# Packed attention, SwiGLU and a bilinear layer on one core: weight sums in more steps, with loads at other places of the queue

## The chip, the cores and the metric

The kernel runs on one core of a Trainium2 chip. The metric is the device time of one launch in microseconds (us), as the median of several runs. All five engines of the core work on one program: TensorE (PE, with its weight loads PEld), VectorE (DVE), ScalarE (ACT), GpSimd (POOL) and SyncE (SP), and every transfer between device memory and the core's buffers is issued from SP's one queue.

## What is computed

```python
p_packed = softmax_attention(p, k, v)          # 8 batches, 8 heads, 32 packed rows, head size 64
a = softmax_attention(q, p_packed, p_packed)   # 576 rows per batch, 4608 tokens of 512 in all
xn = a / rms(a) * rms_g
h = silu(xn @ w_gate) * (xn @ w_val)           # 512 -> 1536
y = h @ w_out                                  # 1536 -> 512
out = ((y @ w1) * (y @ w2)) @ w3 @ w_out2      # 512 -> 1024 -> 1024 -> 512
```

Every large product is done with operands cut into a high and a low float32r part, as three products (high by high, low by high, high by low). The product w3 @ w_out2 is folded into one matrix beforehand, and y @ w1 and y @ w2 are done with seven block products in place of eight (a Strassen-like scheme), for which sums and differences of weight blocks and of y's blocks are needed.

## The kernel before

The program has three stages, one behind the other on TensorE.

**Attention and h.** Up to about 528 us the attention, the norm and h are computed, batch by batch, and h is stored transposed in device memory (`hT_d`).

**y and the preparation of the second layer.** y is computed in nine tiles of 512 tokens by `y_part(t, tag)` (line 557). I call them tile 0 to tile 8. A tile has 12 steps (one per 128 rows of w_out), and a step is 12 matmuls (line 566, four PSUM banks by three products). In step n of all tiles the kernel also issues the load of the h row n+4 (`fetch_h`, tile `hr`, five buffers) and splits row n+2 (`split_h`): ScalarE writes the high part `hh` (line 55), VectorE the low part `hl` (line 56), each with three buffers. So the split of a row can start when the row three ahead of it has been multiplied, and must be done two steps later. At a tile's end two evictions each on ScalarE and VectorE write `y`, which goes to `y_d` three steps later (`store_later`, `stores`).

Between tiles stand the two halves of the folded product, `folded(0)` after tile 2 and `folded(1)` after tile 4 (96 matmuls each, line 657), which read the converted and split w3 and w_out2.

Beside the tiles other work is handed out by `together(main, total, *others)`: each of the others is a generator with a number of pieces, and a first and a last place as shares of the main work; after each step at most one piece is taken, from whichever is furthest behind. The order in which the instructions are written is the order in each engine's queue; nothing is reordered later. The pieces beside tiles 5 to 7 are those of `layer2()`, 33 of them: 16 conversions of 64-bit weight blocks (`w64` loaded, ScalarE and VectorE two operations each, GpSimd one at line 114) and four groups of sums. A group takes four converted blocks a11, a12, a21, a22 (tiles `c_o`), forms sums and differences of them in place on GpSimd (lines 608 to 616), splits seven results into a staging buffer with `put` (high part on ScalarE, low part on VectorE, 128x512 each) and stores them as four transfers of 896 KB to `ws_d`. There are two staging buffers, `stage0` and `stage1`.

Then come, at the top level of the program:

```python
    together(chained(y_part(5, "gv"), y_part(6, "at"), y_part(7, "gv")), 36.0, (33, layer2(), 0.0, 0.97))
    flush()
    p2_ctx.close()
    ...
    fetch_y(0)
    load_w(0)
    together(y_part(NTILE - 1, "at"), 12.0, (8, sums(0), 0.0, 0.85), (4, last_loads(0), 0.1, 0.9))
```

`flush()` issues all stores still held. `p2_ctx.close()` gives the staging buffers' memory to new tiles. `fetch_y(0)` loads y tiles 0 and 1 (`yi`, 1 MB each) and `load_w(0)` the first slice of the summed weights (`w`, 1.8 MB). `sums(0)` (line 709) forms y's sums for the first pair of tiles, with parts `xh` on ScalarE and `xl` on VectorE (two of seven on GpSimd); these tiles lie where the staging buffers lay, so their first writes wait for the last stores out of `stage1`. `last_loads(n)` loads and splits four blocks of the folded matrix (`w34_h`, `w34_l`).

**The second layer.** `run(p)` (line 780) works through pairs of y tiles: for each of eight slices i, seven block products (42 matmuls, line 799), and the products into the output (line 772). ScalarE copies the first product's bank to `p1` (line 805) before TensorE may add to that bank. In the first pair, each slice ends with one piece of `last_loads(1)`.

Of the kernel before, what the change touches and what calls it, by code (L numbers as in the profile page):

```python
# [13 lines left out]
ALU = mybir.AluOpType  # L14
# [18 lines left out]
def packed_attention_swiglu_bilinear(ctx: ExitStack, tc, qT, kT, v, pT, rms_g, w_gv, w_out,  # L33
                                     w1, w2, w3T, w_out2, out):
    nc = tc.nc
# [561 lines left out]
    def group(g):  # L597
# [5 lines left out]
        def put(j, src, eng):  # L603
            hi, lo = (to[:, :, j, s, :] for s in range(2))
            split(hi, lo, src.rearrange("p (i n) -> p i n", i=4), eng)

        put(3, a22, nc.vector)
        nc.gpsimd.tensor_tensor(out=a22, in0=a21, in1=a22, op=ALU.add)
        put(0, a11, nc.vector)
        nc.gpsimd.tensor_tensor(out=a21, in0=a11, in1=a21, op=ALU.subtract)  # L610
        yield
        nc.gpsimd.tensor_tensor(out=a11, in0=a22, in1=a11, op=ALU.subtract)
        put(1, a12, nc.vector)
        put(4, a22, nc.vector)
        yield
        nc.gpsimd.tensor_tensor(out=a12, in0=a12, in1=a11, op=ALU.subtract)
        put(6, a21, nc.vector)
# [57 lines left out]
    late = chained(late, last_split())  # L675
    together(chained(y_part(3, "at"), y_part(4, "gv"), folded(1, "at")), 32.0, (8, late, 0.0, 0.7))
    together(chained(y_part(5, "gv"), y_part(6, "at"), y_part(7, "gv")), 36.0, (33, layer2(), 0.0, 0.97))
    flush()
    p2_ctx.close()
    cv2_ctx.close()  # L680

    wt = ctx.enter_context(tc.tile_pool(name="wt", bufs=1, side="right"))
    pairs = [(t, t + 1) for t in range(0, NTILE - 1, 2)] + [(NTILE - 1,)]
    ys, xs, ws = {}, {}, {}

    def fetch_y(p):
        if p < len(pairs):  # L690
# [54 lines left out]
    def last_loads(n):  # L745
        for kk in range(4 * n, 4 * n + 4):
            split(w34_h[kk], w34_l[kk], fetch(w34_d[128 * kk:128 * kk + 128, :]), nc.gpsimd)
            yield

    fetch_y(0)  # L750
    load_w(0)
    together(y_part(NTILE - 1, "at"), 12.0, (8, sums(0), 0.0, 0.85), (4, last_loads(0), 0.1, 0.9))
    flush()
# [26 lines left out]
    def run(p):  # L780
# [7 lines left out]
        for i in range(8):  # L788
# [98 lines left out]
```

## Time and profile before

| | |
|---|---|
| median of 3 runs | 1455.12 us (1455.07 to 1457.11) |
| the profiled execution | 1451.91 us |
| its span, first to last instruction | 1450.1 us |
| TensorE busy | 1360.0 us, 94% |
| VectorE, ScalarE, GpSimd busy | 55%, 38%, 34% |
| transfers' share of the 16 DMA engines | 49.5% |
| mean granted TensorE clock | 0.981 |

The profile shows one execution. TensorE is busy almost throughout, so the places that matter are the few at which it waits. They are found in the timeline of its instructions, where a wait stands in brackets behind the instruction that ended it, and by laying the starts of equal pieces of work beside each other: two tiles with the same 144 matmuls should take equally long.

### The profile page before, as it was taken

Reading aid. Unit: us, or ns where it says so; the run is one execution under the profiler, and the core shown is the slowest. Engines: PE = TensorE matmul, PEld = TensorE weight load, DVE = VectorE, ACT = ScalarE, POOL = GpSimd, SP = SyncE. Lnnn points to the kernel's source line nnn. Section 1 sums busy time; section 2 is a strip of 40 time slices with the busy share of each in tenths; the row PEclk is TensorE's granted clock in tenths of the full one; section 3 lists DMA queues with packets and bytes.
Section 4 is the critical chain, followed back from the end, with each engine's and each line's share of the span. In section 5 each row is a group of like instructions: output and inputs, shape, how many; then the busy total and the mean of one; then the engine's idle time right before and its main releaser. Section 6 shows DMA issues by size and latency. Waiting matters only on the chain.

```text
span 1450.1 us, 22603 instructions
## 1 busy us (share of the span) xinstructions
PE 1360.0 (94%) x8824; PEld 1121.8 (77%) x8824; DVE 795.9 (55%) x1267; ACT 546.7 (38%) x1080; POOL 489.9 (34%) x438
## 2 busy tenths in 40 slices
PE   4579999999999899999999978999999999999988
PEld 2368878778788788888887756888788788788877
DVE  4787576666766557736358844335334433533343
ACT  3455455555555555624245532113112211311211
POOL 2456445445456542201034503322221222222111
PEclk9689999999999999999999999999999999999999
DMA  9854453444222466726349885442642633444263
GB/s 308 296 186 119 160 186 120 154 153 141 75 96 81 153 211 236 229 98 201 121 161 364 313 307 225 167 149 84 238 146 88 237 141 115 179 142 145 92 254 125
DMA packets 65562, 253.65 MB, mean 175 GB/s; under 512 B 7344, under 2 KB 7344, under 8 KB 55344
## 3 DMA queue, kind: packets, MB, share of 16 engines
q1 hardware_dynamic: 65456, 252.21, 49.5%
q8 instruction: 69, 1.13, 0.3%
q14 instruction: 37, 0.30, 0.1%
HBM read 185.08 MB, written 67.11 MB: 174 GB/s over the span
## 4 chain that ended last, share of the span: by engine, by line
PE 75%; DVE 8%; DMA 5%; ACT 3%; issue 3%; POOL 1%; SPq 1%; ACTq 0%; DVEq 0%; POOLq 0%
PE gv L799 22%; PE gv L376 17%; PE at L566 8%; PE gv L772 7%; PE at L772 7%; PE gv L566 6%; PE at L337 2%; DMA hr<-w_d 2%; DMA w<-ws_d 2%; PE at L657 2%; PE gv L657 2%; DVE stage L56 1%; PE at L292 1%; DVE c_t L111 1%; DVE th L383 1%
## 5 line engine op out<-in xcount | busy, mean ns | idle before, releaser
L799 PE MATMUL gv<-xh,w 128*128 128x512 f32 (+1 forms) x1120 | 288.7, 373 | 13.5 <-DMA w<-ws_d 6.1
L55 ACT ACTIVATE hh<-hr 128x512 fp32r<-128x512 f32 (+1 forms) x148 | 91.2, 618 | 421.1 <-DVE hr L767 332.9
L799 PEld LDWEIGHTS gv<-xh,w 128*128 128x128 f32 x1120 | 201.9, 190 | 53.3 <-DMA w<-ws_d 7.4
L388 POOL TENSOR_TENSOR ht<-th,vl 128x288 f32<-128x288 f32 x192 | 163.8, 861 | 178.6 <-ACT vl L387 97.6
L376 PE MATMUL gv<-ah,wbh 128*128 128x288 f32 x768 | 178.6, 314 | 15.9 <-ACT vl L387 12.4
L56 DVE TENSOR_TENSOR hl<-hr,hh 128x512 fp32r<-128x512 f32 (+1 forms) x148 | 140.4, 951 | 63.2 <-ACT hh L55 60.2
L376 PEld LDWEIGHTS gv<-ah,wbh 128*128 128x128 f32 x768 | 122.7, 191 | 67.6 <-issue 27.8
L826 POOL TENSOR_TENSOR u<-u,c 128x512 f32<-128x512 f32 (+1 forms) x40 | 63.5, 1587 | 323.5 <-DVE u L767 323.5
L376 PE MATMUL gv<-al,wbh 128*128 128x288 f32 x768 | 167.2, 299 | 0.0
L767 DVE TENSOR_TENSOR hr<-gv,hr 128x512 f32<-128x512 f32 (+1 forms) x80 | 51.1, 639 | 209.4 <-PE gv L799 209.4
L376 PE MATMUL gv<-ah,wbl 128*128 128x288 f32 x768 | 165.5, 297 | 0.0
L799 PE MATMUL gv<-xl,w 128*128 128x512 f32 (+1 forms) x560 | 162.3, 372 | 0.0
L114 POOL TENSOR_TENSOR c_o<-c_o,c_y 128x512 int32<-128x512 int32 x52 | 72.9, 1402 | 223.1 <-DVE c_o L112 200.6
L376 PEld LDWEIGHTS gv<-al,wbh 128*128 128x128 f32 x768 | 125.1, 190 | 1.1 <-DVE al L56 0.9
L376 PEld LDWEIGHTS gv<-ah,wbl 128*128 128x128 f32 x768 | 124.8, 190 | 0.0
L383 DVE SCALAR_TENSOR_TENSOR th<-th,gv 128x288 f32<-128x288 f32 x192 | 84.3, 445 | 63.1 <-ACT th L382 62.1
L799 PEld LDWEIGHTS gv<-xl,w 128*128 128x128 f32 x560 | 102.6, 191 | 18.4
L566 PE MATMUL at<-hh,wo_h 128*128 128x512 f32 x240 | 94.7, 394 | 7.3 <-ACT hh L55 7.3
L387 ACT ACTIVATE vl<-gv 128x288 f32<-128x288 f32 x192 | 79.3, 413 | 58.5 <-PE gv L376 57.2
L56 DVE TENSOR_TENSOR wbl<-at,wbh 128x512 fp32r<-128x512 f32 x96 | 65.9, 687 | 60.3 <-ACT wbh L55 59.6
L566 PE MATMUL at<-hl,wo_h 128*128 128x512 f32 x240 | 94.8, 395 | 2.3 <-DVE hl L56 2.1
L382 ACT ACTIVATE th<-gv 128x288 f32<-128x288 f32 x192 | 79.4, 413 | 42.9 <-PE gv L376 42.9
(131 smaller groups left out, 2416.2 us busy)
## 6 DMA issues: line engine op xcount, KB each, us to landing
w<-ws_d SPq DMA_DIRECT2D x40, 1792.0 KB, 7.4
hT_d<-ht SPq DMA_DIRECT2D x96, 288.0 KB, 2.5
hr<-hT_d SPq DMA_DIRECT2D x108, 256.0 KB, 4.4
ws_d<-stage SPq DMA_DIRECT2D x16, 896.0 KB, 8.3
w<-in_w_gv_dram SPq DMA_DIRECT2D x24, 512.0 KB, 7.0
w<-in_w_out_dram SPq DMA_DIRECT2D x20, 512.0 KB, 4.5
v<-in_v_dram SPq DMA_DIRECT2D x8, 1152.0 KB, 7.6
q<-in_qT_dram SPq DMA_DIRECT2D x8, 1152.0 KB, 7.0
```

Of the source, the lines that this page charges most:

```text
L55: nc.scalar.activation(out=hi, in_=src, func=AF.Copy)
L56: eng_lo.tensor_tensor(out=lo, in0=src, in1=hi.bitcast(F32), op=ALU.subtract)
L114: nc.gpsimd.tensor_tensor(out=d, in0=d, in1=shape(y), op=ALU.add)
L376: nc.tensor.matmul(t[:, :HALF], lhsT=w[:, e, 256 * i + 128 * f:256 * i + 128 * f + 128], rhs=x[:, e, HALF * hf:HALF * hf + HALF], start=(n ...
L382: nc.scalar.activation(out=th, in_=t[:, :HALF], func=AF.Tanh, scale=0.5)
L383: nc.vector.scalar_tensor_tensor(out=th, in0=th, scalar=1.0, in1=t[:, :HALF], op0=ALU.add, op1=ALU.mult)
L387: nc.scalar.activation(out=vl, in_=t[:, :HALF], func=AF.Copy, scale=0.5)
L388: nc.gpsimd.tensor_tensor(out=ht[:, hf], in0=th, in1=vl, op=ALU.mult)
L566: nc.tensor.matmul(acc[m], lhsT=w[:, kk, 128 * m:128 * m + 128], rhs=x, start=(kk == 0 and a == 0), stop=(kk == NF - 1 and a == 2))
L772: nc.tensor.matmul(acc[m], lhsT=x[:, 128 * m:128 * m + 128], rhs=w[i], start=(i == 0 and n == 0), stop=(i == 7 and n == 2))
L799: nc.tensor.matmul(t, lhsT=wi[:, r, j, a], rhs=x[b][:, j, r, :w], start=(start and n == 0), stop=(n == 5), skip_group_check=True)
L826: nc.gpsimd.tensor_tensor(out=u2, in0=u2, in1=c22, op=ALU.mult)
```

## The change

Three things are edited. (1) In `group`, the seven puts and four GpSimd operations are cut into five pieces in place of four, and a put stands a piece behind the GpSimd operation that it reads. (2) The second half of the folded product moves from behind tile 4 to behind tile 3, with the last conversions for it beside tile 3; `layer2` (now 37 pieces) starts with six pieces beside the second half of tile 4, and its other 31 end at 0.9 of tiles 5 to 7. The loads of `fetch_y(0)` are handed out as one piece at 0.3 to 0.4 of these tiles, and the `flush()` before tile 8 is gone, so that stores still held go out between the next loads. (3) `load_w(0)` becomes a piece of tile 8 at 0.3 to 0.4; `last_loads` issues each load one piece ahead of the split that uses it (five pieces), and in the first pair it starts at the second slice.

```diff
         put(3, a22, nc.vector)
         nc.gpsimd.tensor_tensor(out=a22, in0=a21, in1=a22, op=ALU.add)
+        yield
         put(0, a11, nc.vector)
         nc.gpsimd.tensor_tensor(out=a21, in0=a11, in1=a21, op=ALU.subtract)
-        yield
         nc.gpsimd.tensor_tensor(out=a11, in0=a22, in1=a11, op=ALU.subtract)
+        yield
+        put(4, a22, nc.vector)
         put(1, a12, nc.vector)
-        put(4, a22, nc.vector)
-        yield
         nc.gpsimd.tensor_tensor(out=a12, in0=a12, in1=a11, op=ALU.subtract)
+        yield
         put(6, a21, nc.vector)
         put(5, a11, nc.vector)
         yield
...
-    together(chained(y_part(3, "at"), y_part(4, "gv"), folded(1, "at")), 32.0, (8, late, 0.0, 0.7))
-    together(chained(y_part(5, "gv"), y_part(6, "at"), y_part(7, "gv")), 36.0, (33, layer2(), 0.0, 0.97))
-    flush()
+    together(chained(y_part(3, "at"), folded(1, "gv")), 20.0, (8, late, 0.0, 0.55))
...
+    second = layer2()
+    together(y_part(4, "at"), 12.0, (6, some(second, 6), 0.5, 1.0))
+    together(chained(y_part(5, "gv"), y_part(6, "at"), y_part(7, "gv")), 36.0, (31, second, 0.0, 0.9),
+             (1, (fetch_y(0) for _ in range(1)), 0.3, 0.4))
...
     def last_loads(n):
-        for kk in range(4 * n, 4 * n + 4):
-            split(w34_h[kk], w34_l[kk], fetch(w34_d[128 * kk:128 * kk + 128, :]), nc.gpsimd)
-            yield
-
-    fetch_y(0)
-    load_w(0)
-    together(y_part(NTILE - 1, "at"), 12.0, (8, sums(0), 0.0, 0.85), (4, last_loads(0), 0.1, 0.9))
+        kks = list(range(4 * n, 4 * n + 4))
+        x = fetch(w34_d[128 * kks[0]:128 * kks[0] + 128, :])
+        yield
+        for kk in kks:
+            nx = fetch(w34_d[128 * kk + 128:128 * kk + 256, :]) if kk != kks[-1] else None
+            split(w34_h[kk], w34_l[kk], x, nc.gpsimd)
+            x = nx
+            yield
+
+    def first_w():
+        load_w(0)
+        yield
+
+    together(y_part(NTILE - 1, "at"), 12.0, (8, sums(0), 0.0, 0.85), (5, last_loads(0), 0.1, 0.9),
+             (1, first_w(), 0.3, 0.4))
...
-            if p == 0:
+            if p == 0 and i > 0:
                 next(rest, None)
```

Three places show what this does to the queues. The first is SP's queue where tile 7 ends and tile 8 begins; `hr<-hT_d` is a load of one h row, `hr<-w34_d` of a block of the folded matrix. Before:

```order
L356 DMA ws_d_67<-stage1_6939 128x1792 x4
L356 DMA y_d_66<-y_9519 128x2048
L694 DMA yi_9534<-y_d_66 128x2048
L694 DMA yi_9536<-y_d_66 128x2048
L703 DMA w_9538<-ws_d_67 128x3584
L497 DMA hr_9542<-hT_d_63 128x512
L497 DMA hr_9564<-hT_d_63 128x512
L497 DMA hr_9585<-hT_d_63 128x512
```

And now:

```order
L356 DMA ws_d_67<-stage1_6939 128x1792
L497 DMA hr_9488<-hT_d_63 128x512
L356 DMA ws_d_67<-stage1_6939 128x1792
L497 DMA hr_9507<-hT_d_63 128x512
L497 DMA hr_9537<-hT_d_63 128x512
L356 DMA ws_d_67<-stage1_6939 128x1792
L497 DMA hr_9560<-hT_d_63 128x512
L356 DMA ws_d_67<-stage1_6939 128x1792
L497 DMA hr_9582<-hT_d_63 128x512
L356 DMA y_d_66<-y_9525 128x2048
L497 DMA hr_9601<-w34_d_65 128x512
L497 DMA hr_9603<-hT_d_63 128x512
```

The four stores of the last group lie between h rows, the `yi` loads are no longer here (they stand some 40 rows up, at the seam of tiles 5 and 6), and `w` comes two rows further down.

The second is ScalarE's queue through one group of sums (the last one, into `stage1`), with the h rows' splits (`hh`) between. Before:

```order
L55 ACTIVATE stage1_6939<-c_o_9383 128x4x128
L55 ACTIVATE stage1_6939<-c_o_9295 128x4x128
L55 ACTIVATE hh_9419<-hr_9364 128x512
L55 ACTIVATE stage1_6939<-c_o_9325 128x4x128
L55 ACTIVATE stage1_6939<-c_o_9383 128x4x128
L55 ACTIVATE hh_9442<-hr_9392 128x512
L55 ACTIVATE stage1_6939<-c_o_9355 128x4x128
L55 ACTIVATE stage1_6939<-c_o_9295 128x4x128
L55 ACTIVATE hh_9465<-hr_9417 128x512
L55 ACTIVATE stage1_6939<-c_o_9325 128x4x128
```

And now:

```order
L55 ACTIVATE stage1_6939<-c_o_9331 128x4x128
L55 ACTIVATE hh_9364<-hr_9312 128x512
L55 ACTIVATE stage1_6939<-c_o_9240 128x4x128
L55 ACTIVATE hh_9388<-hr_9340 128x512
L55 ACTIVATE stage1_6939<-c_o_9331 128x4x128
L55 ACTIVATE stage1_6939<-c_o_9273 128x4x128
L55 ACTIVATE hh_9411<-hr_9362 128x512
L55 ACTIVATE stage1_6939<-c_o_9303 128x4x128
L55 ACTIVATE stage1_6939<-c_o_9240 128x4x128
L55 ACTIVATE hh_9433<-hr_9386 128x512
L55 ACTIVATE stage1_6939<-c_o_9273 128x4x128
```

The seven puts now stretch over four h rows in place of three; the GpSimd operations keep their order.

The third is ScalarE's queue at the start of the second layer. Before:

```order
L555 ACTIVATE y_9774<-at_9540 128x512
L555 ACTIVATE y_9774<-at_9541 128x512
L55 ACTIVATE w34_h3_6280<-hr_9779 128x512
L805 ACTIVATE hr_9807<-gv_9804 128x512
L55 ACTIVATE hh_9862<-hr_9851 128x512
L55 ACTIVATE w34_h4_9790<-hr_9866 128x512
L805 ACTIVATE hr_9875<-gv_9872 128x512
L55 ACTIVATE n2_h_9788<-u2_9808 128x512
```

And now:

```order
L555 ACTIVATE y_9770<-at_9535 128x512
L555 ACTIVATE y_9770<-at_9536 128x512
L55 ACTIVATE w34_h2_6278<-hr_9721 128x512
L55 ACTIVATE xh_9556<-yi_8966 128x1024
L55 ACTIVATE w34_h3_6280<-hr_9775 128x512
L817 ACTIVATE hr_9807<-gv_9804 128x512
L55 ACTIVATE hh_9862<-hr_9851 128x512
L817 ACTIVATE hr_9871<-gv_9868 128x512
L55 ACTIVATE n2_h_9788<-u2_9808 128x512
```

The split `w34_h4` is no longer ahead of the second slice's copy (`hr<-gv`, line 805, now 817), and two more operations, `w34_h2` and the last `xh`, stand ahead of the first slice's copy.

## Rows read from the trace of the kernel before

**Rows 1.** Page: busy us, share of the span and instructions of each engine.

```profile
PE 1360.0 (94%) x8824; PEld 1121.8 (77%) x8824; DVE 795.9 (55%) x1267; ACT 546.7 (38%) x1080; POOL 489.9 (34%) x438
```

**Rows 2.** TensorE timeline (start, us, instruction): starts of tiles 1, 2, 5 to 8.

```profile
560.41 0.39 PE L566 MATMUL gv<-hh,wo_h 128*128 128x512 f32 x1
...
593.05 0.39 PE L566 MATMUL at<-hh,wo_h 128*128 128x512 f32 x1
...
734.65 0.39 PE L566 MATMUL gv<-hh,wo_h 128*128 128x512 f32 x1
...
767.92 0.39 PE L566 MATMUL at<-hh,wo_h 128*128 128x512 f32 x1
...
802.17 0.39 PE L566 MATMUL gv<-hh,wo_h 128*128 128x512 f32 x1
...
837.44 0.39 PE L566 MATMUL at<-hh,wo_h 128*128 128x512 f32 x1
```

**Rows 3.** TensorE timeline: first products of pairs 0 and 1, first output products.

```profile
882.22 0.40 PE L799 MATMUL gv<-xh,w 128*128 128x512 f32 x1
...
905.63 0.39 PE L772 MATMUL at<-w_h,hh 128*128 128x512 f32 x1
...
1009.72 0.40 PE L799 MATMUL gv<-xh,w 128*128 128x512 f32 x1
...
1027.19 0.39 PE L772 MATMUL at<-w_h,hh 128*128 128x512 f32 x1
```

**Rows 4.** TensorE timeline: waits in tiles 6, 7, 8 and pair 0.

```profile
783.23 0.50 PE L566 MATMUL at<-hl,wo_h 128*128 128x512 f32 x1 [1.32 <-DVE hl L56]
...
809.15 0.50 PE L566 MATMUL gv<-hl,wo_h 128*128 128x512 f32 x1 [1.15 <-DVE hl L56]
...
852.46 0.80 PE L566 MATMUL at<-hh,wo_h 128*128 128x512 f32 x1 [6.70 <-ACT hh L55]
...
901.19 0.73 PE L799 MATMUL gv<-xh,w 128*128 128x512 f32 x2 [3.64 <-ACT hr L805]
```

**Rows 5.** ScalarE timeline at the start of tile 8.

```profile
850.83 1.06 ACT L55 ACTIVATE xh<-yi 128x1024 fp32r<-128x1024 f32 x1 [12.56 <-DMA yi<-y_d]
851.80 0.61 ACT L55 ACTIVATE hh<-hr 128x512 fp32r<-128x512 f32 x1
```

**Rows 6.** SP's queue there: start and length of runs of issues.

```profile
834.44 3.01 SPq L356 DMA_DIRECT2D ws_d<-stage  x4
838.40 0.36 SPq L356 DMA_DIRECT2D y_d<-y  x1
838.80 2.54 SPq L694 DMA_DIRECT2D yi<-y_d  x2
844.78 0.32 SPq L703 DMA_DIRECT2D w<-ws_d  x1
```

**Rows 7.** ScalarE timeline in pair 0.

```profile
900.03 0.63 ACT L55 ACTIVATE w_h<-hr 128x512 fp32r<-128x512 f32 x1 [6.19 <-DMA hr<-w_d]
```

**Rows 8.** Timelines through a group in tile 6: ScalarE, GpSimd, VectorE.

```profile
780.98 0.63 ACT L55 ACTIVATE stage<-c_o 128x512 fp32r<-128x512 f32 x1 [1.07 <-POOL c_o L612]
...
781.02 1.60 POOL L616 TENSOR_TENSOR c_o<-c_o 128x512 f32<-128x512 f32 x1
...
781.41 1.76 DVE L56 TENSOR_TENSOR hl<-hr,hh 128x512 fp32r<-128x512 f32 x1
```

**Rows 9.** VectorE's splits, 735 to 882 us (ns minimum/median/maximum, first and last start).

```profile
L56 DVE TENSOR_TENSOR hl<-hr,hh x46: 677/690/2893, 736.1 to 875.9; 128x512 fp32r<-128x512 f32 x46
...
L56 DVE TENSOR_TENSOR xl<-yi,xh x5: 1210/1226/1227, 851.9 to 878.9; 128x1024 fp32r<-128x1024 f32 x5
```

**Rows 10.** Stretches: engines' busy us, granted clock, DMA share, GB/s at the end.

```profile
740.00:745.00 5.00, 5.00 (x24) 4.14 (x23) 3.40 (x5) 3.35 (x6) 2.59 (x2) 1.00 0.98 300
...
768.00:802.00 34.00, 32.68 (x145) 26.75 (x144) 25.77 (x33) 19.14 (x35) 16.27 (x12) 1.00 1.01 391
...
850.00:855.00 5.00, 1.99 (x4) 1.29 (x5) 2.96 (x3) 1.66 (x3) 0.00 (x0) 0.58 1.04 441
```

More of the change, by code (lines that the diff above doesn't have):

```diff
@@ L608, in group @@
         nc.gpsimd.tensor_tensor(out=a22, in0=a21, in1=a22, op=ALU.add)
+        yield
         put(0, a11, nc.vector)
         nc.gpsimd.tensor_tensor(out=a21, in0=a11, in1=a21, op=ALU.subtract)
+        nc.gpsimd.tensor_tensor(out=a11, in0=a22, in1=a11, op=ALU.subtract)
         yield
-        nc.gpsimd.tensor_tensor(out=a11, in0=a22, in1=a11, op=ALU.subtract)
+        put(4, a22, nc.vector)
         put(1, a12, nc.vector)
-        put(4, a22, nc.vector)
+        nc.gpsimd.tensor_tensor(out=a12, in0=a12, in1=a11, op=ALU.subtract)
         yield
-        nc.gpsimd.tensor_tensor(out=a12, in0=a12, in1=a11, op=ALU.subtract)
         put(6, a21, nc.vector)
@@ L675, in packed_attention_swiglu_bilinear @@
     late = chained(late, last_split())
-    together(chained(y_part(3, "at"), y_part(4, "gv"), folded(1, "at")), 32.0, (8, late, 0.0, 0.7))
-    together(chained(y_part(5, "gv"), y_part(6, "at"), y_part(7, "gv")), 36.0, (33, layer2(), 0.0, 0.97))
-    flush()
-    p2_ctx.close()
-    cv2_ctx.close()
-    wt = ctx.enter_context(tc.tile_pool(name="wt", bufs=1, side="right"))
+    together(chained(y_part(3, "at"), folded(1, "gv")), 20.0, (8, late, 0.0, 0.55))
     pairs = [(t, t + 1) for t in range(0, NTILE - 1, 2)] + [(NTILE - 1,)]
@@ L698, in fetch_y @@
                 ys[p] = [x[:, :, :TT // 2], x[:, :, TT // 2:]]
+    second = layer2()
+    together(y_part(4, "at"), 12.0, (6, some(second, 6), 0.5, 1.0))
+    together(chained(y_part(5, "gv"), y_part(6, "at"), y_part(7, "gv")), 36.0, (31, second, 0.0, 0.9),
+             (1, (fetch_y(0) for _ in range(1)), 0.3, 0.4))
+    p2_ctx.close()
+    cv2_ctx.close()
+    wt = ctx.enter_context(tc.tile_pool(name="wt", bufs=1, side="right"))
     def load_w(n):
```

## The prediction

> **What bounds the kernel now.** The page comes first: TensorE is busy for 1360.0 of the span's 1450.1 us [rows 1], so it is the bound, and a change that removes no matmul can only win back time in which it waits or runs at the lower clock. Next its timeline, read by starts of equal work. Tile 1 takes 593.05 - 560.41 = 32.64 us [rows 2] with seven conversions beside it: that is a clean tile, 2.72 us a step. Tile 5 takes 33.27, tile 6 34.25, tile 7 35.27 and tile 8 44.78 us (from 837.44 to pair 0's start at 882.22) [rows 2, 3]. The excesses are 0.63, 1.61, 2.63 and 12.14 us. Pair 0 needs 23.41 us from its first product to its first output product, pair 1 for the same 17.47 [rows 3]: excess 5.94 us. In all 22.95 us lie in the stretch that the change touches, 1.6% of the run. What ended the waits is in the brackets [rows 4]: VectorE's low split of an h row in tiles 6 and 7, ScalarE's high split after 6.70 us in tile 8, ScalarE's copy after 3.64 us in pair 0. [...]
>
> **Tile 8: why ScalarE was late.** ScalarE stood 12.56 us at the first `xh`, whose input is the load of `yi`; the h row's split behind it in the queue ran only at 851.80 [rows 5]. The queue of SP shows why the load was late: four stores of 896 KB, `y_d`, and only then the two `yi` loads, at 838.80 [rows 6], all in one burst. The `w` load, which waits for those stores, was issued at 844.78, so the last store landed some 7.3 us after the burst of stores ended at 837.45.
>
> After the change `yi` is loaded some 40 us earlier and drops out. But `xh` lies on the staging buffer's memory and still waits for the last `ws_d` store, and it still stands ahead of an h row's split (row 99). So the wait is not removed, it changes its releaser, and the sum is when that store lands. Call T tile 8's start. The last store is in SP's queue right behind the load of row 101, which needs a buffer freed by row 96's low split. That split starts when row 93 is multiplied, two steps before T (T - 5.4), and takes 0.61 on ScalarE [rows 5] and 0.69 on VectorE [rows 9]: the store is issued near T - 4. With the 7.3 us above, from a fuller queue, it lands by T + 3.3; with the queue less full I take T + 2. ScalarE is there from T + 0.7 (evictions and row 98's split done). Then `xh` 1.06, row 99's split 0.61, VectorE's `xl` 1.23 [rows 9] and low split 0.69 beside and behind it: row 99 is done at T + 5.0, or T + 6.3 for the late landing, and is needed at T + 8.2, three steps in. Row 100 has a difference (the size of `xl`, 1.23), an `xh`, its own split, `xl` and a low split ahead, 4.8 us more: T + 9.8, or T + 11.1, against T + 10.9. So the margin is 1.1 us, or a stall of 0.2 at the late end. From there on seven `xh` (7.4 us) and twelve splits (7.4 us) on ScalarE lie within 32.6 us, and the engines catch up. The `w` load waits in SP's queue for what is by then long done, and stands ahead of row 105's load, which has four steps of room. I keep 0.5 us of excess: **gain 11.6**, bounds 5 (late store, below) and 12.14.
>
> **Pair 0.** ScalarE stood 6.19 us at `w34_h4`, a split that waits for a load issued in the same piece, ahead of the second slice's copy [rows 7]; TensorE waited 3.64 us for that copy [rows 4]. Now the load goes out in the second slice and its split stands at the end of the third, a slice of some 12 us later, with its user two slices on; nothing is left ahead of the copy that waits for a load. What is put there instead: `w34_h2`, the last `xh` and `w34_h3` stand between the evictions and the first copy, 0.63 + 1.06 + 0.63 = 2.3 us where 0.63 stood. TensorE needs that copy only at its fourth product, 18 matmuls or 4.1 us after 882.22; ScalarE ends its last eviction 0.8 us after that mark, and the copy (0.6) would end at 3.7. A margin of 0.4: cost nothing, and at most 1 us if the cover is gone. GpSimd's last `xl` moves about 5 us later, and TensorE reads it in the seventh product, 9 us in. **Gain 5.5**, bounds 3.6 (the wait alone, with the copy's margin lost) and 5.94.
>
> **Tiles 5 to 7.** In a group, ScalarE waits at a put for the GpSimd operation just written (1.07 us for line 612), and VectorE's split of an h row takes 1.76 us while GpSimd's 1.60 us addition runs [rows 8], against a median of 0.69 [rows 9]. So VectorE loses about a GpSimd operation's length for each. Before, a group has four steps, 10.9 us, and asks of VectorE eleven splits by 0.69 = 7.6 plus four times 1.6 = 6.4, in all 14.0: 3.1 us too much. A split runs about one step (2.7 us) ahead of its use, so some stall is left per group, as the rows show. Now five steps, 13.6 us, ask 8.3 + 6.4 = 14.7: too much by 1.1, which the 2.7 of lead covers. The groups also no longer meet the evictions at a tile's end, and ScalarE waits for no addition of its own piece. I leave one stall of 1.1 us: **gain 3.8**, bounds 0 and 4.87.
>
> [...]
>
> **What is moved at no cost.** Tile 3 now holds seven conversions, as tile 1 does in a clean 32.64 us [rows 2]; tile 4 holds five, and GpSimd and the queue are idle enough there. The `yi` loads add 2.1 MB at the seam of tiles 5 and 6. By the order of the program SP issues 11.5 MB in tile 6 (11.0 before), and 391 GB/s were moved there with all DMA engines busy [rows 10]: 29.5 us of 32.6. A load of an h row has some 12 us between issue and use. Cost 0, bounds 0 and 3.
>
> **Sum.** 11.6 + 5.5 + 3.8 = 20.9 us off the profiled execution's 1451.9 gives 1431.0. The median of the runs lies 3.2 above that execution (1455.1), and I carry that over: **1434.2**.
>
> **Rivals.** (a) *VectorE stays short in tiles 5 to 7.* The lead of one step is eaten by the transfers being late, and the four stalls remain. For it: these stretches have all DMA engines busy [rows 10]. Against it: 14.7 against 13.6 is a third of the old overload. 1434.2 + 3.8 = 1438.0.
>
> (b) *The last store takes `yi`'s place in tile 8.* If SP reaches the store only in tile 8's second step, as the program writes it, it lands near T + 10 and row 99 at T + 13: 4.8 us late, times 12.14/8.1 for the clock (8.1 being all waits of tile 8 in its timeline, 6.70 the largest) is 7.2, less the 0.5 kept: 1440.9. Against it: SP runs ahead of TensorE, held only by buffers.
>
> (c) *Pair 0's wait moves to another slice.* The split behind a load now ends the third slice, and a late load would hold the fourth copy as before: 1434.2 + 5.5 = 1439.7. For it: the second pair's `yi` loads and a `w` are on the way then; against it: a whole slice between.
>
> [...]
>
> (e) *It does not do what it says:* GpSimd's operations keep their order, and the stalls of tiles 5 to 8 together shift into tile 8, whose pieces now include a `w` load in front of h rows. Then only pair 0's gain is left with losses against it: about 1453, no change.
>
> **Chances.** Forecast 0.70, (a) 0.11, (b) 0.09, (c) 0.04, (d) 0.03, (e) 0.03. A measurement of this kernel can tell some 0.2%, or 2.9 us, from no change: faster 0.94, same 0.03, slower 0.03. The range takes in everything gained (1455.1 - 22.95 = 1432.2, less 3 us if the offset between profile and median is not carried over) and the ends of (a) to (c) with a little for two of them at once: 1429 to 1444.
>
> **What would show it.** In the new trace: tiles 5 to 7 near 32.7 us each, with at most one wait for `hl`; ScalarE's first `xh` in tile 8 released by a store of `ws_d`, near T + 2, and tile 8 under 34 us with the clock at 1.00; pair 0 near 17.5 us to its first output product, without a wait for line 817's copy. [...]

## The result, and the profile after

The changed kernel takes **1434.01 us** (median of 4 runs, 1431.36 to 1435.77) where the kernel before took 1456.11 on the same chip (4 runs, 1455.07 to 1457.72): a ratio of 0.9846, with a 95% interval from 0.9825 to 0.9866. The forecast was 1434.2. The profiled execution took 1431.36, its span is 1429.2, that is 20.9 us under the 1450.1 of before.

The page of the changed kernel, its span, the engines' busy time (beside [rows 1]) and the head of the chain that ended last:

```profile
span 1429.2 us, 22605 instructions
...
PE 1353.3 (95%) x8824; PEld 1119.0 (78%) x8824; DVE 787.5 (55%) x1267; ACT 545.7 (38%) x1080; POOL 489.7 (34%) x438
...
PE 80%; DVE 7%; ACT 3%; DMA 3%; issue 2%; POOL 0%; SPq 0%; DVEq 0%; ACTq 0%; POOLq 0%
```

The number of matmuls and of the other engines' operations is the same; what is gone is waiting. Where it is gone from is read by starts of equal work, as before. TensorE's timeline of the changed kernel at the start of tile 8, of pair 0 and of pair 0's first output product (start, us, instruction), beside [rows 2, 3]:

```profile
832.13 0.39 PE L566 MATMUL at<-hh,wo_h 128*128 128x512 f32 x1
...
866.49 0.63 PE L811 MATMUL gv<-xh,w 128*128 128x512 f32 x2
...
884.27 0.39 PE L784 MATMUL at<-w_h,hh 128*128 128x512 f32 x1
```

By such starts the stretch of the change reads so:

| | before | after | gained | forecast |
|---|---|---|---|---|
| tiles 5, 6, 7 | 33.27, 34.25, 35.27 | 32.64, 32.64, 32.64 | 4.87 | 3.8 |
| tile 8 | 44.78 | 34.36 | 10.42 | 11.6 |
| pair 0 to its first output product | 23.41 | 17.78 | 5.63 | 5.5 |
| sum | | | 20.92 | 20.9 |

The sum is the whole difference of the spans (in the rest 0.44 us gained ahead of tile 5 and 0.46 lost behind pair 0's first output product cancel). In tiles 5 to 8 one wait in brackets is left, in tile 8, and the granted clock stays at 1.00 through it. The stretches table (us, busy us of PE, PEld, DVE, ACT and POOL, granted clock, DMA share, GB/s) and the wait in TensorE's timeline, beside [rows 4, 10]:

```profile
734.20:832.10 97.90, 97.90 (x433) 81.11 (x432) 77.33 (x95) 54.71 (x95) 43.68 (x28) 1.00 0.88 333
832.10:866.40 34.30, 33.41 (x145) 26.83 (x144) 22.07 (x21) 13.58 (x20) 5.41 (x3) 1.00 0.59 220
```

```profile
844.82 0.50 PE L566 MATMUL at<-hl,wo_h 128*128 128x512 f32 x1 [0.84 <-DVE hl L56]
```

In tiles 5 to 7 TensorE is busy for all of the 97.90 us. In tile 8 the bracket holds only 0.84 of the 1.72 us above a clean tile; by the starts of the matmuls the rest is in short gaps, 0.3 us of it at the low split before, at 840.73. For tile 8's wait the releaser to look for is behind ScalarE's first `xh`, beside [rows 5]. ScalarE's timeline of the changed kernel there, and in pair 0 (beside [rows 7]):

```profile
837.76 1.06 ACT L55 ACTIVATE xh<-yi 128x1024 fp32r<-128x1024 f32 x1 [4.80 <-DMA ws_d<-stage]
...
867.18 0.62 ACT L55 ACTIVATE w_h<-hr 128x512 fp32r<-128x512 f32 x1
867.70 1.05 ACT L55 ACTIVATE xh<-yi 128x1024 fp32r<-128x1024 f32 x1
868.65 0.62 ACT L55 ACTIVATE w_h<-hr 128x512 fp32r<-128x512 f32 x1
869.17 0.59 ACT L817 ACTIVATE hr<-gv 128x512 f32<-128x512 f32 x1
```

As forecast, the first `xh` no longer waits for `yi` but for the last store out of the staging buffer. It starts 5.6 us behind tile 8's start T (837.76 - 832.13), though, not 2 to 3.3. In pair 0 the two `w_h` and the `xh` stand in front of the first copy (line 817), the copy ends at 869.76, and TensorE waits for none of them.

SP's queue in the changed kernel, beside [rows 6]:

```profile
828.05 1.25 SPq L356 DMA_DIRECT2D ws_d<-stage  x1
829.39 0.46 SPq L497 DMA_DIRECT2D hr<-hT_d  x1
829.89 1.59 SPq L356 DMA_DIRECT2D ws_d<-stage  x1
831.58 1.07 SPq L497 DMA_DIRECT2D hr<-hT_d  x1
833.08 0.96 SPq L356 DMA_DIRECT2D y_d<-y  x1
```

The last store's issue starts at 829.89, T - 2.2, and ends at 831.48; `xh` starts 6.3 us after that end.

### The profile page after: what moved, and what is told of

Its sections match the earlier page's. It is cut to its first block, busy times and chain, and to the rows that moved or that the text cites. A ratio compares the mean times of both kernels' runs of the same rounds, so it can differ in the third digit from the quotient of the medians.

```text
span 1429.2 us, 22605 instructions
## 1 busy us (share of the span) xinstructions
PE 1353.3 (95%) x8824; PEld 1119.0 (78%) x8824; DVE 787.5 (55%) x1267; ACT 545.7 (38%) x1080; POOL 489.7 (34%) x438
## 4 chain that ended last, share of the span: by engine, by line
PE 80%; DVE 7%; ACT 3%; DMA 3%; issue 2%; POOL 0%; SPq 0%; DVEq 0%; ACTq 0%; POOLq 0%
PE gv L811 24%; PE gv L376 17%; PE at L566 13%; PE gv L784 7%; PE at L784 7%; PE gv L566 5%; PE gv L658 3%; PE at L337 2%; DMA w<-ws_d 2%; DVE th L383 1%; PE at L292 1%; DVE a L274 1%; DVE wbl L56 1%; DVE wgv L112 1%; ACT vl L387 1%
## 5 line engine op out<-in xcount | busy, mean ns | idle before, releaser
L56 DVE TENSOR_TENSOR hl<-hr,hh 128x512 fp32r<-128x512 f32 (+1 forms) x148 | 130.2, 883 | 60.3 <-ACT hh L55 57.7
L811 PEld LDWEIGHTS gv<-xl,w 128*128 128x128 f32 x560 | 102.1, 190 | 18.3
L566 PE MATMUL at<-hl,wo_h 128*128 128x512 f32 x288 | 112.3, 390 | 0.9 <-DVE hl L56 0.8
L566 PE MATMUL at<-hh,wo_h 128*128 128x512 f32 x288 | 112.2, 390 | 0.0
L566 PE MATMUL at<-hh,wo_l 128*128 128x512 f32 x288 | 112.1, 389 | 0.0
L387 ACT ACTIVATE vl<-gv 128x288 f32<-128x288 f32 x192 | 79.4, 414 | 58.6 <-PE gv L376 56.1
L56 DVE TENSOR_TENSOR wbl<-at,wbh 128x512 fp32r<-128x512 f32 x96 | 65.9, 686 | 60.4 <-ACT wbh L55 59.8
```

What stands on the lines that cost most here:

```text
L56: eng_lo.tensor_tensor(out=lo, in0=src, in1=hi.bitcast(F32), op=ALU.subtract)
L387: nc.scalar.activation(out=vl, in_=t[:, :HALF], func=AF.Copy, scale=0.5)
L566: nc.tensor.matmul(acc[m], lhsT=w[:, kk, 128 * m:128 * m + 128], rhs=x, start=(kk == 0 and a == 0), stop=(kk == NF - 1 and a == 2))
L811: nc.tensor.matmul(t, lhsT=wi[:, r, j, a], rhs=x[b][:, j, r, :w], start=(start and n == 0), stop=(n == 5), skip_group_check=True)
```

## Experiments

All tile lengths below are taken from starts as above. Two kernels were profiled twice with the same code, once here and once later on one chip with the other: tile 8 came out at 34.36 and 34.38, and at 32.68 and 32.67, and the first `xh` at T + 5.63 and 5.64, and at T + 3.92 both times. Tile 6 came out at 32.64 and 33.03, and at 32.64 and 33.05. Two further kernels, in the section on pair 0, differ only behind tile 8: their tile 6 is 33.29 and 32.64, their tile 8 37.03 and 37.06. So a difference up to 0.7 us in tiles 5 to 7 means nothing here, tile 8 repeats to 0.03, and the whole run varies by some us. The theory is the prediction's: four causes, each with its own gain. The rivals ask, for each, whether another part of the change did it.

### Tiles 5 to 7: more steps, or GpSimd a step ahead

Four pieces in each group of sums in place of five, and 27 pieces in place of 31 behind tile 4:

```diff
         nc.gpsimd.tensor_tensor(out=a22, in0=a21, in1=a22, op=ALU.add)
-        yield
         put(0, a11, nc.vector)
         nc.gpsimd.tensor_tensor(out=a21, in0=a11, in1=a21, op=ALU.subtract)
+        yield
         nc.gpsimd.tensor_tensor(out=a11, in0=a22, in1=a11, op=ALU.subtract)
-        yield
+        put(1, a12, nc.vector)
         put(4, a22, nc.vector)
-        put(1, a12, nc.vector)
+        yield
         nc.gpsimd.tensor_tensor(out=a12, in0=a12, in1=a11, op=ALU.subtract)
-        yield
         put(6, a21, nc.vector)
...
-    together(chained(y_part(5, "gv"), y_part(6, "at"), y_part(7, "gv")), 36.0, (31, second, 0.0, 0.9),
+    together(chained(y_part(5, "gv"), y_part(6, "at"), y_part(7, "gv")), 36.0, (27, second, 0.0, 0.9),
```

> The changed kernel with the groups of sums back in four pieces, as before; layer2 then has 33 pieces, 6 beside tile 4 and 27 that end at the same 0.9 of tiles 5 to 7. My theory is that VectorE's time per group decides: four steps ask 14.0 us of it in 10.9 us, so the waits for the low split come back at the end of each group, about 1 us each, tiles 5 to 7 lose 2 to 4.9 us together against 32.64 us each in the changed kernel, and the run is 1436 to 1439 us. The rival: what emptied these tiles is the earlier start and the distance of the groups from the evictions, not the fifth piece; then tiles 5 to 7 stay within 0.3 us of clean and the run is at 1434 us.

Measured: 1431.93 us (1431.13 to 1433.65), ratio to before 0.9852 [0.9836, 0.9868]. Tiles 5 to 8: 34.00, 33.44, 33.22, 32.65. The waits for VectorE's `hl` are back, the first in TensorE's timeline of this kernel at

```profile
743.85 0.50 PE L566 MATMUL gv<-hl,wo_h 128*128 128x512 f32 x1 [1.02 <-DVE hl L56]
```

So the old groups lose 2.74 us (100.66 against 97.92). By the starts of the matmuls nearly all of it lies at those that use a low split or stand right behind one; the two waits in brackets are 1.02 and 0.29 us, the rest is in gaps too short for a bracket. This edit takes away the fifth step and GpSimd's lead together; the next run parts the two. The other 2.13 of the 4.87 gained come with four groups of four steps as well; four of the 16 conversions and the first piece of a group now lie beside tile 4, and the groups end at 0.9, and I did not part these two. The run as a whole is not slower than the changed kernel, in part because tile 8 became clean: the last store's issue starts at 831.46, T - 3.5, and the first `xh` at 838.51, T + 3.6. Tile 8 thus depends on when the last stores go out, which is taken up below.

The group's third and fourth GpSimd operation at their old distance, one step before their `put`s in place of two, with five pieces:

```diff
         nc.gpsimd.tensor_tensor(out=a21, in0=a11, in1=a21, op=ALU.subtract)
+        yield
         nc.gpsimd.tensor_tensor(out=a11, in0=a22, in1=a11, op=ALU.subtract)
-        yield
+        put(1, a12, nc.vector)
         put(4, a22, nc.vector)
-        put(1, a12, nc.vector)
+        yield
         nc.gpsimd.tensor_tensor(out=a12, in0=a12, in1=a11, op=ALU.subtract)
-        yield
         put(6, a21, nc.vector)
```

> The changed kernel with five pieces per group, but GpSimd's third and fourth operation each at the head of the piece after the one where the change has it. If the fifth piece does all (VectorE's time per step, wherever GpSimd's operation stands), tiles 5 to 7 stay at 32.6 to 32.9 us each and the run is at 1434 us. The rival, that GpSimd a piece ahead is what keeps ScalarE and so the low splits from waiting, gives waits for the low split in tiles 5 to 7 of 0.5 to 1.3 us per group, 2 to 5 us in all, 1436 to 1439 us.

Measured: 1434.39 us (1432.46 to 1434.73), 0.9862 [0.9848, 0.9877]; tiles 32.64, 32.64, 32.90, 34.07. The 0.26 us more in tile 7 are no more than tile 6 varies by itself: the lead of these two operations is worth nothing that shows. So the fifth step, with the first operation's lead that comes with it, is the difference of the two runs, 100.66 - 98.18 = 2.48 us. Where VectorE's time goes shows in the groups of instructions by line, tiles 5 to 7 (operation, count, busy us, mean ns, idle before). First the changed kernel, then this one:

```profile
L56 DVE TENSOR_TENSOR hl<-hr,hh 128x512 fp32r<-128x512 f32 x36 | 30.3, 842 | 13.2 <-ACT hh L55 13.2
L56 DVE TENSOR_TENSOR stage<-c_o,stage 128x512 fp32r<-128x512 f32 x28 | 28.3, 1034 | 5.5 <-ACT stage L55 5.5
```

```profile
L56 DVE TENSOR_TENSOR hl<-hr,hh 128x512 fp32r<-128x512 f32 x36 | 34.8, 969 | 11.5 <-ACT hh L55 11.5
L56 DVE TENSOR_TENSOR stage<-c_o,stage 128x512 fp32r<-128x512 f32 x28 | 25.0, 916 | 5.5 <-ACT stage L55 5.5
```

The two splits together take 58.6 us there and 59.8 here. With the additions written earlier an h row's split takes 842 ns in the mean in place of 969, and a staging buffer's 1034 in place of 916, so that their sum is nearly the same. Of the edit's two halves only the fifth step gave anything that shows.

### Tile 8: which of the moved loads

`yi` loaded at the seam again, right ahead of tile 8, all else as changed:

```diff
-    together(chained(y_part(5, "gv"), y_part(6, "at"), y_part(7, "gv")), 36.0, (31, second, 0.0, 0.9),
-             (1, (fetch_y(0) for _ in range(1)), 0.3, 0.4))
+    together(chained(y_part(5, "gv"), y_part(6, "at"), y_part(7, "gv")), 36.0, (31, second, 0.0, 0.9))
+    fetch_y(0)
```

> The changed kernel with the two yi loads put back between tiles 7 and 8, and still no flush there, so the last two stores of the staging buffer come behind them in the queue. If the early yi loads are what saved tile 8, its first xh waits for yi or for the stores behind it until 9 to 14 us into the tile, and tile 8 grows from 34.4 to 38 to 45 us: the run 1438 to 1445 us. The rival, that the place of the w load and of the h rows behind it was the cost and yi only the last to land, leaves tile 8 below 36 us and the run at 1434 to 1436 us.

Measured: 1436.19 us (1435.53 to 1437.3), 0.9878 [0.9863, 0.9893]; tile 8 38.28, all else as changed. ScalarE's first `xh` in this kernel:

```profile
841.29 1.06 ACT L55 ACTIVATE xh<-yi 128x1024 fp32r<-128x1024 f32 x1 [8.61 <-DMA hr<-hT_d]
```

It starts at T + 9.4, with T = 831.85. SP's queue has the last store of this kernel at

```profile
829.04 0.44 SPq L356 DMA_DIRECT2D ws_d<-stage  x1
```

that is at T - 2.8, earlier than in the changed kernel (T - 2.2). But the two `yi` loads stand ahead of it, and `xh` starts 12.25 us behind the start of its issue in place of 7.87 (837.76 - 829.89): by that I put its landing near 841.2, though the bracket names a load of an h row. The prediction's rival (b) put `xh` behind a store about as late, but by a late issue; here, by this reading, it is the landing that is late. But tile 8 is longer by 3.92 us, not by the 10 that the old tile 8 would need. The early `yi`, to which the sum gave nearly all of tile 8's gain, is a part of it.

The flush ahead of tile 8 put back, so that the last stores are issued at the end of tile 7 and not when their own countdown lets them:

```diff
              (1, (fetch_y(0) for _ in range(1)), 0.3, 0.4))
+    flush()
```

> The changed kernel with the flush before tile 8 kept: yi is loaded early, but the stores go out in one burst, and y_d, which waits for tile 7's last eviction, stands ahead of the loads of rows 100 and on. By my theory the last store lands earlier (about 2 us into tile 8, not 5.6), so the first xh comes earlier, and row 100's load is issued some 2 us into the tile, late but in time: tile 8 33 to 35 us, the run at 1433 to 1436 us. The rival, that the flush was a large part of the old wait since it holds back h rows, gives a wait for a load of an h row in tile 8 of 2 us or more, tile 8 above 37 us and the run above 1437 us.

Measured: 1430.85 us (1430.78 to 1431.63), 0.9842 [0.9827, 0.9857]. Tile 8 is 32.68, a clean one. SP's queue and ScalarE's first `xh` in this kernel (T = 835.01):

```profile
828.64 0.75 SPq L497 DMA_DIRECT2D hr<-hT_d  x1
829.44 2.72 SPq L356 DMA_DIRECT2D ws_d<-stage  x2
835.96 0.32 SPq L356 DMA_DIRECT2D y_d<-y  x1
```

```profile
838.93 1.06 ACT L55 ACTIVATE xh<-yi 128x1024 fp32r<-128x1024 f32 x1 [3.09 <-DMA ws_d<-stage]
```

With the flush the last two stores go out together, ahead of an h row's load that the changed kernel puts between them, and `xh` starts at T + 3.9 in place of T + 5.6. The flush that the change took out, and that the prediction did not price, was worth 1.68 us.

Now the old seam as a whole: the flush, then `yi`, then `w`, before tile 8, with the new groups and the new order of w34's loads.

```diff
-    together(chained(y_part(5, "gv"), y_part(6, "at"), y_part(7, "gv")), 36.0, (31, second, 0.0, 0.9),
-             (1, (fetch_y(0) for _ in range(1)), 0.3, 0.4))
+    together(chained(y_part(5, "gv"), y_part(6, "at"), y_part(7, "gv")), 36.0, (31, second, 0.0, 0.9))
+    flush()
...
-    together(y_part(NTILE - 1, "at"), 12.0, (8, sums(0), 0.0, 0.85), (5, last_loads(0), 0.1, 0.9),
-             (1, first_w(), 0.3, 0.4))
+    fetch_y(0)
+    load_w(0)
+    together(y_part(NTILE - 1, "at"), 12.0, (8, sums(0), 0.0, 0.85), (5, last_loads(0), 0.1, 0.9))
```

> The changed kernel with the whole old seam before tile 8: flush, the two yi loads, the w load, then the tile. If the seam alone makes tile 8's loss, whatever stands before and after, tile 8 is back at 43 to 46 us with a wait of 5 to 8 us for a high split and a granted clock below 0.7 in the 5 us behind it, and the run is 1443 to 1447 us. If part of the gain came from the earlier end of the groups, tile 8 is 38 to 42 us.

Measured: 1435.63 us (1434.21 to 1440.84), 0.9887 [0.9859, 0.9914]; tile 8 39.13. Of the two outcomes that were expected the second came: the old seam alone brings back 6.5 of the old 12.1 us above a clean tile. Its waits in TensorE's timeline:

```profile
842.65 0.51 PE L566 MATMUL at<-hh,wo_h 128*128 128x512 f32 x1 [1.95 <-ACT hh L55]
...
849.12 0.49 PE L566 MATMUL at<-hh,wo_h 128*128 128x512 f32 x1 [1.03 <-ACT hh L55]
```

There are two waits for `hh`, not one. To see what the second is, the same with `yi` early, so that only the flush and `w` stand at the seam:

```diff
              (1, (fetch_y(0) for _ in range(1)), 0.3, 0.4))
+    flush()
...
-    together(y_part(NTILE - 1, "at"), 12.0, (8, sums(0), 0.0, 0.85), (5, last_loads(0), 0.1, 0.9),
-             (1, first_w(), 0.3, 0.4))
+    load_w(0)
+    together(y_part(NTILE - 1, "at"), 12.0, (8, sums(0), 0.0, 0.85), (5, last_loads(0), 0.1, 0.9))
```

> The changed kernel with flush and the w load back before tile 8, and only the yi loads early. The w load waits for the last store, and the loads of rows 100 and on stand behind it. If yi alone was the old cost, tile 8 stays below 35.5 us, the run at 1433 to 1436 us. If the w load's place was a second one, hidden behind yi's wait, row 100 is loaded only some 5 us into the tile and lands behind 1.8 MB of w, TensorE waits 2 to 5 us for it, tile 8 is 36 to 40 us and the run 1436 to 1440 us.

Measured: 1435.92 us (1434.66 to 1437.83), 0.9878 [0.9859, 0.9896]; tile 8 37.42. SP's queue, ScalarE's wait and TensorE's in this kernel:

```profile
839.48 0.32 SPq L708 DMA_DIRECT2D w<-ws_d  x1
839.85 1.44 SPq L497 DMA_DIRECT2D hr<-hT_d  x3
```

```profile
848.30 1.98 ACT L55 ACTIVATE hh<-hr 128x512 fp32r<-128x512 f32 x3 [3.70 <-DMA hr<-hT_d]
```

```profile
848.98 0.50 PE L566 MATMUL at<-hh,wo_h 128*128 128x512 f32 x1 [2.41 <-ACT hh L55]
```

The first `xh` is at 839.45, T + 3.9, as early as with the flush alone; but SP stands at the `w` load until 839.48, because it waits for the last store, and three h rows' loads are issued only behind it, with the 1.8 MB of `w` on the way. That costs 4.74 us (37.42 against 32.68). In the kernel before, I take it, most of this lay behind the wait for `yi`: `w` was issued at 844.78 [rows 6], the first `xh` started only at 850.83 [rows 5], and of a second wait 0.64 us are left in TensorE's timeline of before:

```profile
859.00 0.50 PE L566 MATMUL at<-hh,wo_h 128*128 128x512 f32 x1 [0.64 <-ACT hh L55]
```

### Tile 8: what the old seam doesn't bring back

The old seam as above, with the 31 pieces ending at 0.97 as of old:

```diff
-    together(chained(y_part(5, "gv"), y_part(6, "at"), y_part(7, "gv")), 36.0, (31, second, 0.0, 0.9))
+    together(chained(y_part(5, "gv"), y_part(6, "at"), y_part(7, "gv")), 36.0, (31, second, 0.0, 0.97))
```

> The seam before tile 8 as it was of old (flush, then yi, then w) gave a tile 8 of 39.13 us, though the old kernel's was 44.76. Here the 31 pieces behind y also end as late as of old (at 0.97 of tiles 5 to 7 in place of 0.9), so that the last four groups' adds and stores lie some 6.9 us nearer to the seam (0.07 of 98 us). Theory L, the groups' end carries the missing 5.6 us, because the last ws_d stores leave later and yi's first use waits for them: tile 8 is 43 to 45.5, and ScalarE's first xh comes 3 us or more after the 8.65 behind tile 8's start that it had. Theory O, w34's loads a piece ahead carry it: tile 8 stays at 38.5 to 40. If both carry a part: between 40 and 43. Tiles 5 to 7 stay within 0.7 of 97.9 in all.

Measured: 1440.65 us (one run, beside 1452.79 of before); tiles 5 to 7 97.92, tile 8 43.46. First `xh` and TensorE's wait in this kernel (T = 834.58), which read almost like [rows 4, 5]:

```profile
847.50 1.06 ACT L55 ACTIVATE xh<-yi 128x1024 fp32r<-128x1024 f32 x1 [12.08 <-DMA yi<-y_d]
```

```profile
849.13 0.80 PE L566 MATMUL at<-hh,wo_h 128*128 128x512 f32 x1 [6.22 <-ACT hh L55]
```

`xh` starts 12.9 us behind T in place of 8.65, and tile 8 grows by 4.33 us. So the end of the groups, 0.9 in place of 0.97, had a large part of tile 8's gain, as long as `yi` stands behind the stores.

The old seam, the groups ending at 0.9, with w34's loads as of old, each fetched and split in one piece (so four pieces in place of five):

```diff
-        kks = list(range(4 * n, 4 * n + 4))
-        x = fetch(w34_d[128 * kks[0]:128 * kks[0] + 128, :])
-        yield
-        for kk in kks:
-            nx = fetch(w34_d[128 * kk + 128:128 * kk + 256, :]) if kk != kks[-1] else None
-            split(w34_h[kk], w34_l[kk], x, nc.gpsimd)
-            x = nx
+        for kk in range(4 * n, 4 * n + 4):
+            split(w34_h[kk], w34_l[kk], fetch(w34_d[128 * kk:128 * kk + 128, :]), nc.gpsimd)
             yield
```

> The same old seam, the 31 pieces ending at 0.9, but w34's four loads as of old: each fetched and split in the same one of four pieces, where the changed kernel fetches a piece ahead in five. With yi early this edit cost tile 8 2.7 us (37.06 against 34.36), with ScalarE's w_h at 844.20 among the late hh and GpSimd's w_l beside VectorE's hl. Theory O, the loads carry what the seam alone doesn't return: tile 8 is 42 to 45. Theory L, the end of the groups does: tile 8 is 39 to 40. If the loads carry only what they carried with yi early: 41 to 42. Pair 0 stays at 17.8, as its first piece is still taken from the second slice on.

Measured: 1437.57 us (one run); tile 8 39.92, that is 0.79 more than with the new loads; pair 0 17.78. The loads carry little here, by one profiled run of each.

### Pair 0 and w34's loads

The changed kernel with `last_loads` as of old, by the diff just shown and in four pieces, and a piece of it after the first slice too:

```diff
-            if p == 0 and i > 0:
+            if p == 0:
```

> The changed kernel with the loads of the folded matrix's blocks as before: each load in the same piece as its split, four pieces in tile 8, and in the first pair from the first slice on. My theory: ScalarE then waits again for the load of the fifth block ahead of the second slice's copy, TensorE 3 to 4 us for that copy, pair 0 needs 22 to 24 us to its first output product in place of 17.78, and the run is 1438 to 1440 us. The rival: in the old kernel the load was late only because the queue was full after tile 8's delay; then pair 0 stays under 19 us and the run at 1434 to 1435 us.

Measured: 1441.67 us (1440.58 to 1441.95), 0.9915 [0.9898, 0.9932]; pair 0 takes 22.88 us to its first output product, tile 8 37.03. The old wait of [rows 4, 7] is back, in ScalarE's and TensorE's timelines of this kernel:

```profile
887.90 0.63 ACT L55 ACTIVATE w_h<-hr 128x512 fp32r<-128x512 f32 x1 [5.96 <-DMA hr<-w_d]
```

```profile
889.07 1.22 PE L806 MATMUL gv<-xh,w 128*128 128x512 f32 x2 [3.47 <-ACT hr L812]
```

`last_loads` as of old, but taken from the second slice on, as changed (the loop as shown above, four pieces in place of five):

```diff
-    together(y_part(NTILE - 1, "at"), 12.0, (8, sums(0), 0.0, 0.85), (5, last_loads(0), 0.1, 0.9),
+    together(y_part(NTILE - 1, "at"), 12.0, (8, sums(0), 0.0, 0.85), (4, last_loads(0), 0.1, 0.9),
```

> The same as the one before, but the first pair's pieces start at the second slice, as in the change. It tells the two halves of that edit apart. If the later start is enough, because the queue is empty by then, pair 0 is at 17.5 to 18 us to its first output product, no slice after it has a wait of over 0.2 us beyond those of the changed kernel, and the run is at 1434 us. If the load a piece ahead is needed, ScalarE waits for a load in the second slice and the third slice's copy is 2 us or more late: 1436 to 1440 us.

Measured: 1437.45 us (1434.06 to 1438.32), 0.9883 [0.9863, 0.9903]; pair 0 17.75, tile 8 37.06. So the slice alone cures pair 0, and the load a piece ahead, which the prediction counted for pair 0, gives nothing there. It gives 2.70 us in tile 8 (37.06 against 34.36), which no term of the sum had. First `xh` is at T + 5.64 (838.63, T = 832.99), as in the changed kernel. ScalarE, GpSimd and VectorE behind it, from the timelines of this kernel, and the stretch of 5 us there:

```profile
844.20 0.61 ACT L55 ACTIVATE w_h<-hr 128x512 fp32r<-128x512 f32 x1
```

```profile
844.89 1.27 POOL L56 TENSOR_TENSOR w_l<-hr,w_h 128x512 fp32r<-128x512 f32 x1 [22.48 <-ACT w_h L55]
```

```profile
844.95 2.36 DVE L56 TENSOR_TENSOR hl<-hr,hh 128x512 fp32r<-128x512 f32 x2
```

```profile
845.00:850.00 5.00, 3.23 (x10) 2.58 (x11) 4.05 (x5) 0.86 (x2) 1.16 (x1) 0.81 0.58 187
```

In the changed kernel ScalarE's first `w_h` of tile 8 comes at 851.66. Here it stands among the late splits, 0.61 us on ScalarE, and GpSimd's low part of it runs beside VectorE's late `hl`, two of which take 2.36 us in place of the 1.28 in VectorE's timeline of the changed kernel:

```profile
844.08 1.28 DVE L56 TENSOR_TENSOR hl<-hr,hh 128x512 fp32r<-128x512 f32 x2
```
TensorE waits 1.91 us in place of 0.84, and the row of the stretch from 845 to 850 shows a granted clock of 0.81 (the changed kernel's 842 to 847 has 1.00).

### The flush and the changed kernel, side by side

The edit is the flush's line again, and for the second kernel none:

```diff
              (1, (fetch_y(0) for _ in range(1)), 0.3, 0.4))
+    flush()
```

> The changed kernel with the flush before tile 8 kept, run again beside the changed kernel itself on one chip. From the two traces tile 8 is 32.68 against 34.36, all else equal: 1.7 us less, 0.1 per cent of the run. If the trace's difference holds, the ratio is 0.0005 to 0.002 below that of the changed kernel, which may be too little to tell from run to run: medians 1429 to 1433 for this one. If the difference was one of two profiled executions only, tile 8 is above 34 here as well.

> The changed kernel itself, beside the one with the flush kept: tile 8 at 34.4 again, with the first xh 5 to 6 us behind its start; median 1431 to 1436, ratio to the kernel before 0.983 to 0.987.

Measured on one chip: with the flush kept 1430.13 us (4 runs, 1427.36 to 1432.08), 0.9842 [0.9822, 0.9861]; the changed kernel 1434.37 (4 runs, 1432.28 to 1436.5), 0.9877 [0.9859, 0.9895]. Tile 8 is 32.67 and 34.38 again. Of the 3.4 us between the two spans (1426.7 and 1430.1), 1.71 lie in tile 8 and 1.6 in the half-size last pair. There TensorE's first wait for a load of `w` is 3.13 us with the flush and 2.90 without, so the waiting doesn't explain it; the granted clock does differ. Its stretches, 6.6 to 11.6 us behind the last pair's start, with the flush and then without:

```profile
1359.00:1364.00 5.00, 2.49 (x21) 2.50 (x22) 1.36 (x2) 0.72 (x3) 1.38 (x2) 1.00 0.96 356
```

```profile
1360.77:1365.77 5.00, 2.72 (x13) 2.72 (x14) 0.94 (x1) 0.72 (x3) 1.14 (x2) 0.76 0.94 335
```

Whether that part follows the flush is not shown: from pair 0's start to the span's end the six profiles with a flush at the seam take 560.5 to 562.2 us, and the six without it, and with pair 0 as changed, 561.7 to 564.4. The 1.7 us of tile 8 are shown; the median's difference of 4.2 is larger than what the edit explains, and the two intervals still overlap. By both sets of runs the changed kernel with the flush kept has the lowest median of all kernels that were run.

## Why the prediction was right

**Time and direction.** The sum came out to the tenth (20.9 us), but two of its terms were off in opposite directions, by -1.2 and +1.1, so it was closer than its parts, and that is luck. So is the nearness of the median (1434.2 against 1434.01): by medians the gain is 22.1 us beside the runs of before on the same chip, and 18.4 us where the changed kernel was run again (1452.79 to 1434.37). Of the signs that the prediction named for tile 8, an `xh` near T + 2 and a tile under 34 us did not come; those for the other two places did.

**Tiles 5 to 7** (forecast 3.8, measured 4.87). The step that counted VectorE's demand against the group's steps held: five steps leave no wait, four leave 2.74 us of loss, and 2.48 of these come without the lead of the third and fourth operation. The other 2.13 us of the gain have no cause shown. What the working says of ScalarE, that it waits for no addition of its own piece any more, is misread: before, too, each `put` that reads a GpSimd operation stood at least one piece behind it, as the 1.07 us wait of [rows 8] does. The stall of 1.1 us that I left in was not there in this profile (0.4 of it in a second one of the same kernel): by the working's own count the 2.7 us of lead cover the 1.1 that VectorE lacks. That count charged VectorE 1.6 us for each addition, an estimate that no run shows: the 64 splits of tiles 5 to 7 took 62.5 us before and 58.6 in the changed kernel, where 64 at the median of 0.69 [rows 9] make 44.2. That is 18.3 and 14.4 us more, or 1.1 and 0.9 for each of the 16 additions there. Rival (a) is out.

**Tile 8** (forecast 11.6, measured 10.42). The releaser was named rightly, a store of `ws_d`, and that `w` in the middle of tile 8 costs nothing held. The mis-sized term is when that store lands. "The store is issued near T - 4" was off: its issue started at T - 2.2, with an h row's load between it and the store before, and took 1.59 us, which I had not counted. The landing behind that was as chosen: 6.3 us to `xh`, where the 6 of T + 2 and the 7.3 of T + 3.3 were the ends. `xh` came at T + 5.6, row 100's low split at T + 12 (844.08) where TensorE wanted it at T + 10.9, and the excess was 1.72 in place of 0.5. What the prediction missed is that the flush, which the change takes out, had sent that store earlier: with it `xh` is at T + 3.9 and tile 8 is clean. Removing the flush stood in no term.

The working gave tile 8's gain to the load of `yi`. The runs show a ladder, each rung one edit: 43.46 with the old seam and the late end of the groups; 39.13 with the groups ending at 0.9; 37.42 with `yi` early; 32.68 with `w` moved into the tile; 34.36 with the flush gone. The first rung down from the old 44.78 is 1.32. The timelines show where it lies: the first wait is 6.70 us before and 6.22 in the kernel of 43.46, and the second, of 0.64 us for `hh` and 0.22 for `hl` before, is in no bracket there. Which edit did that is open; w34's loads cost 0.79 in one run with the groups ending at 0.9, but its waits differ from those with the new loads by 0.03 us at most. So of the gain `yi` has 1.71 on this path, the groups' end 4.33 and the place of `w` 4.74, and the flush's removal took 1.68 back; each rung is one or two profiled runs. The parts depend on the order: with `w` already moved and no flush, `yi` at the seam costs 3.92. The prediction's total was right because it asked when the last thing that `xh` and the h rows need is there, and not because it knew which edit brought it forward.

**Pair 0** (forecast 5.5, measured 5.63). The wait named was the one, and the longer row of work in front of the first copy cost nothing. But of the two edits that the working named together, the start a slice later alone does it (17.75 us without the other); the load a piece ahead works in tile 8, for 2.70 us. Rival (c) is out: no `w_h` waits for a load ahead of a copy.

**Moved at no cost** held: tiles 5 to 7 run clean at a granted clock of 1.00 with 333 GB/s moved. An `xh` as late as rival (b) had it came, without the `w` load at the seam, only in the kernel with `yi` there, and by what I read as a late landing. Rival (e) is refuted by the sum's parts.

## What to carry to other kernels

When several things stand late at one seam, take a ladder of single edits before giving the gain to the longest wait: behind the wait for `yi` stood a second one, for h rows queued behind a load that itself waited for stores. A flush that looks like a stop at the seam can be what sends the last stores early; take it out only if their own countdown lets them go as soon. And when an engine is short by little in a group of steps, one more step of room can do more than another order of the work in it, as it did here (2.48 us against nothing that shows).

## What the runs showed of the hardware

The delay of the first `xh` and the length of tile 8 go together, but not in proportion. With `w` inside the tile and w34's loads a piece ahead the excess above a clean tile is 0.0 for `xh` at T + 3.6 and T + 3.9, 1.7 at T + 5.6, and 5.6 at T + 9.4; with these loads as of old it is 4.4 at T + 5.6. With `w` at the seam it is 4.8 at T + 3.9, 6.5 at T + 8.65 and 10.8 at T + 12.9: the wait for the h rows behind `w` is 2.41, then 1.03, and then in no bracket, so I read it as covered by the first, the more the longer that is.

In three profiles the granted clock at a wait of tile 8 was the lower the longer the wait. After the 0.84 us wait of the changed kernel the clock stayed at 1.00 (842 to 847). With the 1.91 us wait of the kernel that only starts a slice later, the 5 us around it average 0.81. With the 6.22 us wait of the old seam with the late end the stretch of 5 us from 1.9 us behind it shows 0.50:

```profile
851.00:856.00 5.00, 4.88 (x12) 3.26 (x10) 2.14 (x3) 2.04 (x3) 0.00 (x0) 0.50 0.99 397
```

The tiles with the 0.84 and the 1.91 us wait are 1.7 and 4.4 us over a clean one in all. But the length of the wait does not settle it. In the last pair the first wait for `w` and the granted clock 6.6 to 11.6 us behind that pair's start were 3.13 us and 1.00 with the flush kept, and 2.90 and 0.76 in the changed kernel beside it (the stretches shown above); in the changed kernel's first profile they were 2.70 and 0.77, and in the kernel before 2.79 and 0.72:

```profile
1359.72:1364.72 5.00, 2.94 (x16) 2.94 (x17) 1.31 (x2) 0.71 (x3) 1.43 (x2) 0.77 0.98 370
```

```profile
1381.04:1386.04 5.00, 2.85 (x13) 2.85 (x14) 0.93 (x1) 0.70 (x3) 1.12 (x2) 0.72 0.98 373
```

Of these four the longest wait is the one with the clock at 1.00.
